# Token statistics of the first phase on ACT or DVE by the planner's queue ends, with a new pacing table

## The chip, the cores and the metric

The kernel runs on one core of one Trainium2 chip. The metric is the device time of one launch in microseconds; of a kernel, the median of its runs counts. Five engines work side by side, each through its own instructions in the order in which the program holds them: PE (TensorE, the matmuls, with its weight loads), DVE (VectorE), ACT (ScalarE), POOL (GpSimd), and SP, which here only issues DMAs. An instruction starts when those ahead of it on its engine are done and the semaphores that it waits for are there.

## What is computed

An input of 8192 tokens with 448 features is normalized over the features, and two branches start from the result: a spectral filter over the 8192 tokens (a real FFT, a small complex two-layer network on each frequency with a soft threshold behind it, the inverse FFT), and a GEGLU network of width 1792.

```
xn = (x - mean(x)) / sqrt(var(x) + 1e-5)          # per token, 448 features
s  = irfft2(soft(W2 . relu(W1 . rfft2(xn) + b1) + b2))   # 4 blocks of 112 features
g  = silu((gelu(xn @ w_gate) * (xn @ w_up)) @ w_down)
out = x + s * g
```

## The kernel before, in words

All of it is matmuls on 16-bit operands that are split in a high and a low part, so that three matmuls replace one of 32 bits. The FFT of 8192 is a product with 128x128 matrices, twiddles and a product over 64. The GEGLU products are done by a seven-product scheme (Strassen-Winograd) on halves of the operands.

**Stages.** The tokens go through the network in 16 chunks of 512, in two passes over the hidden width: pass 0 takes 8 of the 14 blocks of 128 hidden features, pass 1 takes 6. PE goes from one unit of the network to the next almost without a break from the start to the end. The work of the spectral branch is laid in between. Its first phase runs from about 84 to 640 us, one chunk of four token tiles (128 tokens each) every 34 us: `load_x` brings the tile `x4`, `stats` makes mean and variance per token in the tile `st`, `norm_act` normalizes on ACT, `factors` splits and adds up the operands of the seven products (scratch `sf` and `sx`, and `xs` for the plain halves) and stores them to `xts`, from which transposing DMAs bring them back as `xta` and `xtb` for the network, and `stage1` makes the first FFT product and stores it (`ysb` to `t1`). The second phase, to about 1450 us, is the middle of the spectral branch (tiles `va`, `vt`, `zs`, `t`), and the third, `load3` and `tiles3`, is the last inverse product: for each pair of token tiles it brings `u2`, `mt`, the input `x2` and the network's output `g2`, PE makes `bd <- u2,mt`, DVE multiplies the product into `g2`, DVE or POOL adds `x2`, and SP stores the result to `out`. The last chunk of the network takes the other way round: the inverse product waits in `s4`, and the network's own last step (`left`, then the silu on ACT into `th`, times `s4`, plus `x2`) ends with stores `out <- th`.

**Units.** A unit of the network handles two blocks of hidden features of a chunk. PE fills `bx` and `by` by products with `xta` (a1, a5, a6, a2 ...) and `xtb` (a3, a4); ACT copies (`by <- bx`, `u <- by`), DVE adds (`v <- bx,u`, `by <- bx,u`), ACT makes the gelu, and the results go as high and low 16-bit halves into `h`, on which the products with `dw` and `wt` (the down projection, into `bd`, `by` and `bx`) work. In pass 1 the weight tile `wt7` lends its space for the unit's 32-bit values, and `wt6` holds sums of halves of them: `wt <- wt` are the sums, `h <- wt,h` and `wt <- wt,wt` the low halves. 

**What sets the order.** Nothing in the program is ordered by hand. The order is written by a planner (`Pace`) while the program is built. It runs the parts above as coroutines against estimates: `cost` gives each operation a duration, `pace.free[e]` is the time at which the planner sees the queue of engine `e` end, and each instruction lands in its engine's queue at the moment when the planner reaches it. `calm(e)` holds a coroutine until the planner sees engine `e` free. `B` and `A` choose DVE or POOL, and ACT or POOL, by the earlier planned end. The table `STEPS` has a row for every stretch of planned time: its numbers are the allowance for a DMA's landing, how busy an engine may be for `calm` to pass, a factor on all costs of engines other than PE, a bias of the choices of `B` and `A`, and a factor on the distance at which groups of the second and tiles of the third phase are started. `SX`, the ring of `sx`, has two buffers, the ring of `g2` two, that of `th` three. SP's DMAs go over eight lanes, and each waits for the landing of the one eight before it.

`stats` is the function in which the code changes. Before, all four token tiles of a chunk go through `bn_stats` and `bn_aggr` on DVE; POOL makes the reciprocal root from the variances.

## Time and profile before

| | us |
|---|---|
| median of 3 runs | 1727.75 (1726.9 to 1728.06) |
| the profiled execution, its own time | 1729.31 |
| its span, first to last instruction | 1727.2 |
| PE busy | 1709.1 (99% of the span), 15654 matmuls |
| DVE busy | 1345.0 (78%), 2317 instructions |
| ACT busy | 1103.3 (64%), 2242 instructions |
| POOL busy | 1014.2 (59%), 1410 instructions |
| granted PE clock | 0.998 |

The profiled execution is 1.56 us above the median, and 2.1 us of its time lie outside its span. "Busy" is the time in which an engine executes instructions; the rest is waiting. In the chain of work that ended last PE has 87%, DVE 6%, and ACT, DMA and POOL 2% each.

### The profile page before, as it was taken

What the parts mean: (1) busy time and instruction counts of PE and PEld (TensorE: products, weight loads), DVE (VectorE), ACT (ScalarE), POOL (GpSimd) and SP (SyncE); (2) the same over time, 40 slices, a digit from 0 to 9 for tenths busy, and PEclk for the clock granted to TensorE, in tenths of its full rate; (3) what the DMA queues carried; (4) which work ended last, traced back from release to release, by engine and by line L of the source; (5) the groups of instructions that cost most, each with busy time, mean ns of one, the idle gap of its engine ahead of it and who ended that gap; (6) DMA issues with size and microseconds to landing.
All of it is one profiled execution on the core that took longest, in us unless ns stands there. A gap on an engine that the chain in (4) does not pass through costs nothing.

```text
span 1727.2 us, 41012 instructions
## 1 busy us (share of the span) xinstructions
PE 1709.1 (99%) x15654; PEld 1435.5 (83%) x15654; DVE 1345.0 (78%) x2317; ACT 1103.3 (64%) x2242; POOL 1014.2 (59%) x1410
## 2 busy tenths in 40 slices
PE   9999999999999999999999999999999999999998
PEld 4447677766777999998999999999999999889886
DVE  8998888778777878778786777787776786577776
ACT  6767766676756657678676667777676665333333
POOL 2487656677735785456374466654555654555556
PEclk9999999999999999999999999999999999999999
DMA  7348986997756753253535875454645544999996
GB/s 275 119 154 256 276 237 207 265 281 202 231 163 189 208 135 77 60 128 88 131 91 172 214 174 122 123 135 109 156 123 137 120 105 123 280 321 314 296 306 229
DMA packets 438308, 316.62 MB, mean 183 GB/s; under 512 B 305792, under 2 KB 409600, under 8 KB 436320
## 3 DMA queue, kind: packets, MB, share of 16 engines
q1 hardware_dynamic: 437824, 313.99, 64.4%
q8 instruction: 122, 2.00, 0.5%
q14 instruction: 74, 0.61, 0.1%
q10 hardware_dynamic: 288, 0.03, 0.0%
HBM read 137.93 MB, written 108.25 MB: 143 GB/s over the span
## 4 chain that ended last, share of the span: by engine, by line
PE 87%; DVE 6%; ACT 2%; DMA 2%; POOL 2%; issue 1%; SPq 0%; POOLq 0%; DVEq 0%; ACTq 0%
PE bd L290 35%; PE bx L290 30%; PE by L290 22%; DMA prt<-th 1%; DVE st L290 1%; ACT wt L290 1%; DVE raws L290 0%; POOL st L290 0%; DVE ysb L290 0%; DVE wt L290 0%; DVE dw L290 0%; DVE left L290 0%; DVE u L290 0%; DMA xta<-xts 0%; DVE h L290 0%
## 5 line engine op out<-in xcount | busy, mean ns | idle before, releaser
L290 PEld LDWEIGHTS <-wt 128*128 128x128 f16 x9142 | 885.4, 98 | 160.2 <-issue 8.2
L290 PE MATMUL bx<-xta,wt 128*128 128x256 f16 (+1 forms) x2819 | 354.0, 275 | 3.5 <-ACT by L290 2.6
L290 PEld LDWEIGHTS <-h 128*128 128x128 f16 x2711 | 259.8, 98 | 75.5 <-POOL h L290 1.6
L290 PE MATMUL by<-xtb,wt 128*128 128x256 f16 x2080 | 255.2, 273 | 0.4 <-DVE by L290 0.3
L290 PE MATMUL bd<-dw,h 128*128 128x448 f16 (+1 forms) x1536 | 243.1, 306 | 1.0 <-DVE ysb L290 0.7
L290 POOL TENSOR_TENSOR wt<-wt 128x256 f32<-128x256 f32 x181 | 140.2, 775 | 94.0 <-DVE wt L290 84.7
L290 PE MATMUL bx<-xtb,wt 128*128 128x256 f16 x1248 | 154.3, 274 | 2.2 <-DVE v L290 2.2
L290 PE MATMUL by<-xta,wt 128*128 128x256 f16 (+1 forms) x899 | 123.8, 282 | 0.1
L290 POOL TENSOR_TENSOR h<-wt,h 128x512 f16<-128x512 f32 (+1 forms) x92 | 96.1, 1058 | 35.9 <-ACT h L290 35.4
L290 DVE TENSOR_TENSOR by<-bx,u 128x512 f32<-128x512 f32 x104 | 72.4, 696 | 52.9 <-PE bx L290 44.9
L290 ACT ACTIVATE u<-by,fc 128x512 f32<-128x512 f32 (+1 forms) x118 | 73.6, 636 | 51.5 <-PE by L290 49.4
L290 PE MATMUL bx<-left,wt 128*128 128x256 f16 x816 | 99.9, 272 | 0.0
L290 DVE TENSOR_TENSOR v<-bx,u 128x512 f32<-128x512 f32 x104 | 71.4, 686 | 36.1 <-PE bx L290 35.5
L290 PE MATMUL bd<-dw,wt 128*128 128x224 f16 (+1 forms) x816 | 97.6, 264 | 0.5 <-DVE left L290 0.5
L290 POOL CAST zs<-t 112x256 f16<-112x256 f32 (+2 forms) x45 | 21.3, 474 | 123.1 <-DVE t L290 107.9
L290 ACT COPY u<-by 128x512 f32<-128x512 f32 x104 | 60.8, 585 | 50.2 <-PE by L290 49.4
L290 ACT CAST h<-wt 128x512 f16<-128x512 f32 (+1 forms) x128 | 68.5, 536 | 31.4 <-DVE wt L290 25.1
L290 PE MATMUL bd<-w2t,wn 113*128 113x112 f16 (+1 forms) x1152 | 77.6, 212 | 0.0
L290 ACT COPY by<-bx 128x512 f32<-128x512 f32 x104 | 59.8, 575 | 21.1 <-PE bx L290 20.8
L290 PE MATMUL bd<-wt,h 128*128 128x224 f16 x603 | 72.0, 259 | 0.8 <-POOL h L290 0.8
L290 PEld LDWEIGHTS <-wn 113*128 113x128 f16 (+1 forms) x1152 | 69.1, 97 | 2.1
L290 DVE SCALAR_TENSOR_TENSOR u<-by,fc,u 128x512 f32<-128x512 f32 (+1 forms) x86 | 55.2, 656 | 18.7 <-PE by L290 12.9
(283 smaller groups left out, 3764.8 us busy)
## 6 DMA issues: line engine op xcount, KB each, us to landing
xts<-sx SPq DMA_DIRECT2D x32, 480.0 KB, 3.6
x<-in_x SPq DMA_DIRECT2D x17, 896.0 KB, 6.2
t<-ysb SPq DMA_DIRECT2D x64, 224.0 KB, 3.8
prt<-th SPq DMA_DIRECT2D x64, 224.0 KB, 3.2
vt<-va SPq DMA_DIRECT2D x256, 56.0 KB, 2.1
left<-prt SPq DMA_DIRECT2D x64, 224.0 KB, 3.7
u<-t SPq DMA_DIRECT2D x32, 448.0 KB, 6.0
x<-in_x SPq DMA_DIRECT2D x32, 448.0 KB, 6.6
```

What stands on the lines that cost most here:

```text
L290: return self.pace.issue(self.name, kind, out, ins, lambda: fn(out, *args, **kw))
```

## The change

In `stats`, for each token tile, the planner compares the ends of two queues as it sees them. If ACT's end lies more than 0.6 us ahead of DVE's, the statistics of that tile are made on ACT: a Copy over the 448 features with a running sum (into `st`), a small Copy that scales it by -1/448, and a Square with that bias and a running sum, with a buffer of the ring `SX` as the place for the 448 results that nobody needs; two small operations on POOL scale the sums to mean and variance. Otherwise DVE does it as before.

```diff
@@ stats
         for a in range(CH):
+            if pace.free["ACT"] + 0.6 < pace.free["DVE"]:
+                sx = yield from SX.get()
+                yield from calm("ACT")
+                S.activation(sx[:, 0:D], x4[:, a, :], AF.Copy, accum_out=s6[:, a, 0:1])
+                S.activation(s6[:, a, 1:2], s6[:, a, 0:1], AF.Copy, scale=-1.0 / D)
+                yield
+                yield from calm("ACT")
+                S.activation(sx[:, 0:D], x4[:, a, :], AF.Square, bias=s6[:, a, 1:2], accum_out=s6[:, a, 2:3])
+                SX.put(sx)
+                G.tensor_scalar(mv[:, a, 0:1], s6[:, a, 0:1], 1.0 / D, None, op0=ALU.mult)
+                G.tensor_scalar(mv[:, a, 1:2], s6[:, a, 2:3], 1.0 / D, None, op0=ALU.mult)
+                yield
+                continue
             yield from (lull if c < PL else calm)("DVE")
             V.bn_stats(s6[:, a, :], x4[:, a, :])
             V.bn_aggr(mv[:, a, :], s6[:, a, :])
@@ STEPS, the rows up to 100 stay, of the others some two thirds differ
...
-(125, 2.5, 0.15, 1.04, 0.0, 1.0), (150, 2.5, 0.15, 1.04, 0.0, 1.0), (175, 2.5, 0.15, 1.04, 0.2, 1.0),
+(125, 2.5, 0.15, 1.07, 0.0, 0.9), (150, 2.5, 0.15, 1.07, 0.0, 0.9), (175, 2.25, 0.15, 1.04, 0.2, 1.0),
...
-(1725, 2.75, 0.05, 0.94, 0.4, 1.0)
+(1725, 1.25, 0.1, 1.045, -0.5, 1.06)
```

The program has the same 15654 matmuls and the same 886 DMAs. Of the 67 `bn_stats` and `bn_aggr` on DVE 44 each are left: 23 of the first phase's tiles go to ACT, which gains 23 of each of the three operations; POOL gains 46 small ones.

Because the planner now sees other times, the order changes on every engine. Three places show it. The first is ACT at the fifth `by <- bx` copy of the network, which before stands at 204.22 us. Before, in ACT's order, with the semaphores that each instruction waits for (`DMAHW` and a number is the landing on that lane; the number behind a name is that of the tile's copy):

```order
CAST wo<-wst 128x448 [waits DVE_49]
COPY by<-bx 128x512 [waits PE_49]
ACTIVATE ysb<-bd_69 128x2x224 [waits DMAHW5_49,DMAHW4_49,PE_49]
ACTIVATE x_1886,st<-x_1886,st 128x448
CAST wo<-wst 128x448 [waits DVE_49]
COPY u_2420<-by 128x512 [waits PE_49]
```

And now:

```order
ACTIVATE th<-bd_69,ms 128x448 [waits DMAHW4_49,PE_49]
ACTIVATE sx,st<-x_1916 128x448 [waits DMAHW7_49,DMAHW6_49,DMAHW3_49]
ACTIVATE st<-st 128x1 [waits Activation_49]
COPY by<-bx 128x512 [waits PE_49]
CAST wo<-wst 128x448 [waits DVE_49]
COPY u_2408<-by 128x512 [waits PE_49]
ACTIVATE sx,st<-x_1916,st 128x448 [waits Activation_49]
```

The first pass over the token tile now stands right ahead of the copy that PE needs, and it waits for three lanes: the load of `x4`, and the stores from the `sx` buffer that it takes over. Of the 23 first passes 13 wait for a DMA in this way.

The second place is POOL in the last unit of the network, from the last sums (`wt7 <- wt7`) to its end. Before:

```order
TENSOR_TENSOR wt7_83<-wt7_83 128x256 x4
TENSOR_TENSOR h_6804<-wt7_83,h_6804 128x512
TENSOR_TENSOR h_6804<-wt7_83,h_6804 128x256
TENSOR_TENSOR h_6804<-wt7_83,h_6804 128x512
TENSOR_TENSOR g2_24520<-g2_24520,x2_24486 128x448
TENSOR_TENSOR th_24607<-th_24607,x2_24210 128x448
```

And now:

```order
TENSOR_TENSOR wt6_82<-wt7_83,wt6_82 128x512
TENSOR_TENSOR h_6882<-wt7_83,h_6882 128x256
TENSOR_TENSOR th_24296<-th_24296,x2_24411 128x448
TENSOR_TENSOR wt6_82<-wt7_83,wt6_82 128x512
TENSOR_TENSOR g2_24426<-g2_24426,x2_24189 128x448
TENSOR_TENSOR wt7_83<-wt7_83 128x256 x3
TENSOR_TENSOR g2_24426<-g2_24426,x2_24189 128x448
TENSOR_TENSOR wt7_83<-wt7_83 128x256
TENSOR_TENSOR h_6882<-wt7_83,h_6882 128x256
TENSOR_TENSOR h_6882<-wt7_83,h_6882 128x512
```

POOL now also has both of the unit's `wt6` differences, which DVE had before, one addition into `th` and two into `g2` ahead of or among the last sums, and one of its last three `h` operations went to DVE. PE reads the last `h` in its products `bd <- wt,h`, 58 matmuls ahead of its end before, and a group of products earlier now.

The third place is DVE at its end, with SP's last stores. Before:

```order
SCALAR_TENSOR_TENSOR left_1744<-bd1_67,ms_86,left_1744 128x448
SCALAR_TENSOR_TENSOR left_1744<-bd0_66,ms_86,left_1744 128x448
TENSOR_TENSOR th_24719<-th_24719,s4_21439 128x448
SCALAR_TENSOR_TENSOR left_1744<-bx_24708,ms_86,left_1744 128x224
TENSOR_TENSOR th_24696<-th_24696,s4_21439 128x224 x2
```

And now:

```order
SCALAR_TENSOR_TENSOR left_1769<-bx_24787,ms_86,left_1769 128x224
SCALAR_TENSOR_TENSOR g2_24710<-bd0_66,ms_86,g2_24710 128x448
TENSOR_TENSOR th_24773<-th_24773,s4_21531 128x224
TENSOR_TENSOR th_24808<-th_24808,s4_21531 128x448
TENSOR_TENSOR th_24773<-th_24773,s4_21531 128x224
TENSOR_TENSOR th_24808<-th_24808,x2_24336 128x448
SCALAR_TENSOR_TENSOR g2_24710<-bd3_69,ms_86,g2_24710 128x448
TENSOR_TENSOR g2_24710<-g2_24710,x2_24629 128x448
```

Both `u2,mt` products of the last pair of tiles moved to PE's very end: one between the last nine products into `bx` (six of them ahead of it, three behind it), the other behind them as PE's last three matmuls, where before PE ended with `bx <- wt,h`. So DVE's last two operations now belong to `g2`, and SP's last DMA, which was a store `out <- th` of 128x224, is now the store `out <- g2` of 128x896.

## The prediction

> **What bounds the kernel now.** I read the busy times first, then PE's waits, then stretches of 100 us, and last the timeline around each place where PE stood still. The first lines of the page, and three rows of the windows (PE, PEld, DVE, ACT, POOL with the number of instructions, then granted clock, DMA share, GB/s):

> ```profile
> span 1727.2 us, 41012 instructions
> PE 1709.1 (99%) x15654; PEld 1435.5 (83%) x15654; DVE 1345.0 (78%) x2317; ACT 1103.3 (64%) x2242; POOL 1014.2 (59%) x1410
> ...
> 100.00:200.00 100.00, 97.14 (x629) 62.02 (x628) 88.16 (x168) 71.37 (x148) 75.12 (x133) 0.98 0.82 231
> 200.00:300.00 100.00, 98.56 (x779) 75.52 (x777) 85.66 (x153) 68.35 (x134) 62.96 (x108) 1.00 0.77 236
> 500.00:600.00 100.00, 100.00 (x851) 82.53 (x850) 80.55 (x168) 64.90 (x127) 56.16 (x98) 1.00 0.68 187
> ```

> PE is the bound: the change leaves its 15654 matmuls alone, so the time can only move in what PE waits and in what comes after its last matmul. The span has 18 us without PE (1727.2 - 1709.1). DVE is at 80 to 88% in the stretch of the statistics, ACT at 65 to 71%: both have room. PE's waits by cause:

> ```profile
> PE bx L290 <- ACT by L290: 2.6, 2, 1.9
> PE bx L290 <- DVE v L290: 2.2, 2, 1.4
> ...
> PE bd L290 <- POOL h L290: 1.1, 2, 0.8
> ...
> PE bd L290 <- DVE ysb L290: 0.7, 1, 0.7
> ```

> The rows left out, but for small ones, belong to the first 20 us, which the change leaves as they are. In the body stand `by` 2.6, `v` 2.2 and `ysb` 0.7: 5.5 us in five places, which is what there is to gain. `h` 1.1 is at the end.

> The sum is made against the profiled execution's own 1729.31 us (span 1727.2 and 2.1 outside); the median of the runs is 1727.75, so 1.56 is taken off again at the end. A change under 0.2%, 3.45 us, can hardly be told from none.

> **The statistics themselves.** What a token tile costs on each engine stands in rows of before; on ACT they are the same two passes that the kernel makes for another purpose at its start (the page of groups by form, window 23 to 100 us, and the answer on the tile `st`):

> ```profile
> L290 ACT ACTIVATE sx<-x,st 128x448 f16<-128x448 f32 x4 | 2.7, 668 | 0.1
> L290 ACT ACTIVATE sx<-x 128x448 f16<-128x448 f32 x4 | 2.3, 567 | 0.0
> ...
> L290 DVE BATCH_NORM_STATS2 st<-x x67: 593/615/628, 3.6 to 600.0; 128x6 f32<-128x448 f32 x67
> L290 DVE BATCH_NORM_AGGREGATE st<-st x67: 181/182/183, 4.3 to 600.7; 128x2 f32<-128x6 f32 x67
> L290 POOL TENSOR_SCALAR st<-st x44: 193/229/687, 4.6 to 603.8; 128x4 f32<-128x4 f32 x34, 128x1 f32<-128x1 f32 x8, 128x2 f32<-128x2 f32 x2
> L290 ACT ACTIVATE st<-st x9: 185/188/203, 9.7 to 37.6; 128x1 f32<-128x1 f32 x9
> L290 ACT ACTIVATION_READ_ACCUMULATOR sx<-x,st x4: 185/186/187, 25.6 to 38.4; 128x1 f32 x4
> ```

> DVE loses 0.615 + 0.182 = 0.797 us per tile. ACT gains 0.567 + 0.186 for the sum, 0.188 for the small Copy, 0.668 + 0.186 for the squares: 1.80 us. POOL gains 2 x 0.229 = 0.46. For 23 tiles that is DVE -18.3, ACT +41.3, POOL +10.5 us, spread over some 520 us. All of it lies beside PE. ACT rises from about 68% by 8 points (41.3 of 520 us), still under DVE, which falls by 3.5. As busy time I cost it at nothing; the cover is ACT's 30% of idle time.

> The price is in the waits. ACT works in order, and 13 of the 23 first passes wait for DMAs: for the load of `x4` and for the stores of the `sx` buffer that serves as scratch. Queued behind such a pass are the copies `by <- bx` and `u <- by` that PE waits for. Before has the like of it with another DMA, in ACT's and PE's timeline at 150 us, and among ACT's waits between 84 and 620 us:

> ```profile
> 150.24 0.63 ACT L290 ACTIVATE th<-bd,ms 128x448 f32<-128x448 f32 x1 [4.36 <-DMA prt<-th]
> 154.72 0.57 ACT L290 COPY by<-bx 128x512 f32<-128x512 f32 x1
> ...
> 155.35 0.92 PE L290 MATMUL bx<-xta,wt 128*128 128x256 f16 x7 [1.89 <-ACT by L290]
> ...
> ACT th L290 <- DMA prt<-th: 8.2, 3, 4.4
> ```

> ACT stood 4.36 us before a `th` whose buffer was still on its way out, the copy came late, and PE lost 1.89. Three `th` waited so, and one of the three cost PE. If about one or two of the 13 waits are late and one in three reaches PE, that is 0.6 us. The ends are 0 (the planner lets all of them come in time) and 3.8 (two such places). The old 1.89 itself stays: in the new order the same `th` waits for a store on a lane, ahead of the same copy.

> [...]

> **The order that moves with it, in the body.** Two of PE's places lose their cause. At 278 us and at 798 us:

> ```profile
> 273.96 3.42 DVE L290 SCALAR_TENSOR_TENSOR wst<-wst,rowc 128x128 f32<-128x128 f32 x1
> ...
> 278.72 0.68 DVE L290 TENSOR_TENSOR v<-bx,u 128x512 f32<-128x512 f32 x1
> 279.45 1.47 PE L290 MATMUL bx<-xtb,wt 128*128 128x256 f16 x12 [1.44 <-DVE v L290]
> ...
> 795.93 2.27 DVE L290 TENSOR_TENSOR wn<-h,wn 112x512 f16<-112x512 f32 x1
> 799.19 1.47 PE L290 MATMUL bx<-xtb,wt 128*128 128x256 f16 x12 [0.75 <-DVE v L290]
> ```

> In both a long DVE operation stood ahead of the `v` that PE waited for. In the new order the `wst` one stands behind that unit's `v`, and the `wn` one is not ahead of it: -1.44 and -0.75. What is late next there is nothing that I can see within half a microsecond. For `ysb` (0.7) I take half, since DVE has 18 us less to do and its order there is new: -0.35. The second `by` (2.6 - 1.9 = 0.7) and the 0.1 to 0.5 us places stay. Body: -1.44 - 0.75 - 0.35 + 0.6 = -1.9, with ends at -5.5 (all five places go) and +4 (two new ones, none goes). DMAs: the same 886 in another order on SP; their share in the first phase is 0.7 to 0.8, so I cost that at nothing, inside these ends.

> **The end of the program.** This term speaks against the change. The timeline of before, ACT, DVE and POOL from the last unit's `a4` on, PE's one wait, and its last matmuls:

> ```profile
> 1701.87 1.47 PE L290 MATMUL bx<-xtb,wt 128*128 128x256 f16 x12
> 1705.05 1.64 DVE L290 SCALAR_TENSOR_TENSOR wt<-v,fc,wt 128x512 f32<-128x512 f32 x1
> 1706.77 3.54 POOL L290 TENSOR_TENSOR wt<-wt 128x256 f32<-128x256 f32 x4 [0.63 <-DVE wt L290]
> 1710.39 3.33 POOL L290 TENSOR_TENSOR h<-wt,h 128x512 f16<-128x512 f32 x3
> 1713.69 1.51 POOL L290 TENSOR_TENSOR g<-g,x 128x448 f32<-128x448 f32 x1
> 1713.78 1.13 PE L290 MATMUL bd<-wt,h 128*128 128x224 f16 x10 [0.76 <-POOL h L290]
> 1720.20 0.45 PE L290 MATMUL bx<-wt,h 128*128 128x224 f16 x3
> 1721.39 1.48 DVE L290 TENSOR_TENSOR th<-th,s 128x224 f32<-128x224 f32 x2
> 1722.65 1.35 POOL L290 TENSOR_TENSOR th<-th,x 128x224 f32<-128x224 f32 x2 [0.33 <-DVE th L290]
> ```

> POOL's chain from the sums to the last `h` ends at 1713.72, 10.4 us behind `a4` (1703.34), and PE wanted it 0.76 earlier, at 9.6. In the new order POOL also has two additions into `g2`, one ahead of the sums and one among them (1.51 each, as in the row at 1713.69), and ahead of them a `th` and a `wt6`; one `h` of the three (3.33 / 3 = 1.1) is DVE's. I put one addition on the path, and 0.5 for what the others overrun POOL's idle 0.63: 1.51 + 0.5 - 1.1 = 0.9 later, 11.3 behind `a4`. PE has one group of products less in between (the 10 of 1713.78, 1.1) and wants it at 8.5. PE would stand 2.8 us where the two waits for `h` were 1.1 together: +1.7. Ends: +0.4 (the group alone, and the other of the two old waits and half of this one gone) and +2.3 (0.6 more, as when DVE is late with the product that the addition among the sums needs).

> Behind PE's last matmul (1720.65) before needed 6.55 us: `left`, `th`, POOL's addition, a store of 112 KB. In the new order DVE still has, after `left`, one `g2` multiply (0.68), three `th` (0.4, 0.63, 0.4), a `th` plus `x2` (0.63), then the last tile's `g2` multiply and addition (0.68 + 0.63). From 0.2 us ahead of PE's end that is 4.3 us behind it, where before the last store left 3.4 behind (1724.0, POOL's end). And the store is 448 KB, not 112:

> ```profile
> out<-g SPq DMA_DIRECT2D x2, 448.0 KB, 2.5
> out<-th SPq DMA_DIRECT2D x2, 112.0 KB, 1.7
> ```

> 0.9 and 0.8 make +1.7. The ends are +1.35 and +2.45; the upper one has the additions slow, as here, where the same 448 elements took 1.55 us beside POOL and 0.61 without it:

> ```profile
> 1703.07 1.58 POOL L290 TENSOR_TENSOR th<-th,x 128x448 f32<-128x448 f32 x1
> 1703.58 1.55 DVE L290 TENSOR_TENSOR g<-g,x 128x448 f32<-128x448 f32 x1
> ...
> 1709.11 0.61 DVE L290 TENSOR_TENSOR g<-g,x 128x448 f32<-128x448 f32 x1
> ```

> [...]

> **Sum.** -1.9 + 1.7 + 1.7 = +1.5. On the profiled execution's 1729.31 that is 1730.8; less the 1.56 by which it lies above the median, 1729.2: no change that can be told.

> **Rivals.** One, slower: the waits for the scratch buffer and `x4` decide. For it: 13 passes wait, each with PE's copies behind it, and the one such place shown cost 1.89. Against it: two of three late `th` cost PE nothing. It decides from two places on: 3.8 in place of the 0.6, the sum is +4.7 and the time 1732.4. The upper ends of the terms for the program's end (+4.75 in place of 3.4) bring the sum to +2.85 alone, and with one such place more (1.9) to +4.7 again.

> Two, faster: DVE's relief and the new order take away the five places of 5.5 us, nothing comes, and POOL's chain at the end costs only its lower end: -5.5 + 0.4 + 1.35 = -3.75, 1724.0. For it: 500 to 600 us ran with PE at 100.00 and DVE at 80.55, so a stretch of the statistics without a wait is possible. Against it: the 1.89 keeps its cause. If PE's end is met without POOL too, 1722.2.

> Three, nothing: the order is new and the waits are others of the same size, in the body and at the end; 1727.75. That the statistics don't move at all is excluded by the 23 tiles in the order.

> **How the numbers follow.** The forecast has 0.43 (its own range is 1726 to 1731), rival three 0.10, both inside 0.2%: same 0.53. Rival one and its kin 0.25, above 1731.2. Rival two 0.22, below 1724.3. The range leaves out a tenth on each side: below, half of rival two (1722.5), above, the body's two places with the upper ends at PE's end, less what is sure to go (1733.5).

> **What would show it.** ACT busy about 1145 us, DVE about 1327, POOL about 1025. PE's waits by `v` at 278 and 798 us gone, `by` at 153 us still there; a wait of PE for `h` of 2 to 3 us near its end; 8 to 8.5 us from PE's last matmul to the span's end, with a store of 448 KB as the last. Wrong is the forecast if ACT's `sx` rows show waits for DMAs of several microseconds with PE's `by` waits behind them, if PE's waits by `by`, `v` and `ysb` (5.5 us now) fall under 1 or rise over 8, or if PE meets `h` in time.

## The result, and the profile after

The changed kernel takes 1744.57 us (median of 4 runs, 1744.02 to 1745.72), before 1727.9 in the same comparison: a ratio of 1.0100, 95% interval 1.0085 to 1.0114. It is 16.7 us slower, where I had forecast no change with a range up to 1733.5. One execution of the last kernel below (2544.43 us at a granted clock of 0.65) is left out of that kernel's ratio. The head of its page:

```profile
span 1742.6 us, 41112 instructions
PE 1713.1 (98%) x15654; PEld 1435.8 (82%) x15654; DVE 1334.6 (77%) x2312; ACT 1129.2 (65%) x2353; POOL 1007.1 (58%) x1419
```

DVE lost 10.4 us of work, ACT gained 25.9, POOL lost 7.1, where the diff's own operations would make 18.3 less, 41.3 more and 10.5 more: the planner also moved other work between the engines. PE's matmuls are the same 15654. The 15.4 us between the two spans (1742.6 - 1727.2) are in PE's waits, in a lower clock behind some of them, and behind PE's last matmul. Between 84 and 1700 us PE stood still for 15.4 us, before for 6.7. The clock stood at half for 3.41 us twice, before once; each time takes 1.7 us of PE's work. The last unit has 1.5 us more of waiting, and 1.85 more lie behind the last matmul. Together that is 13.7; the remaining 1.7 us I can assign to no place. PE's waits by cause between 84 and 1700 us, the largest of after, then what before has below the rows of the prediction:

```profile
PE bd L290 <- DVE zs L290: 3.3, 2, 1.9
PE bd L290 <- ACT th L290: 2.9, 1, 2.9
PE bx L290 <- ACT by L290: 2.2, 3, 1.1
PE bx L290 <- DVE v L290: 2.1, 2, 1.5
PE bd L290 <- DVE xs L290: 1.1, 2, 0.7
PE bd L290 <- DVE h L290: 1.1, 2, 0.7
```

```profile
PE bd L290 <- DVE left L290: 0.5, 1, 0.5
PE bd L290 <- DVE zs L290: 0.3, 1, 0.3
PE by L290 <- DVE by L290: 0.3, 1, 0.3
```

After, the `th` row is new, and `zs` grew from 0.3 to 3.3. To see where the time goes I set the starts of PE's matmuls in the two traces against the same amount of PE work (columns streamed). After is ahead by 3.7 us when before stands at about 380 us: the waits at 153, 186 and 278 us became fewer, as hoped. It gives 3.2 of that back in small waits up to 550 us, loses 5.8 at one place (550 to 590 us) and 3.7 at another (around 881), about 3 in small pieces up to 1700, and 1.6 in the last unit: PE's last matmul is 13.5 us later.

The first place, ACT and PE in after's timeline, and the granted clock in the windows:

```profile
576.23 0.58 ACT L290 ACTIVATE sx<-x 128x448 f16<-128x448 f32 x1 [5.63 <-DMA xts<-sx]
578.58 0.67 ACT L290 ACTIVATE sx<-x,st 128x448 f16<-128x448 f32 x1
582.84 0.63 ACT L290 ACTIVATE th<-bd,ms 128x448 f32<-128x448 f32 x1
...
578.12 0.36 PE L290 MATMUL bd<-wt,h 128*128 128x224 f16 x2 [0.27 <-ACT h L290]
578.87 0.56 PE L290 MATMUL bd<-wt,h 128*128 128x224 f16 x4 [0.39 <-DVE h L290]
583.52 1.69 PE L290 MATMUL bd<-dw,left 128*128 128x224 f16 x12 [2.94 <-ACT th L290]
...
585.00:590.00 5.00, 5.00 (x37) 4.04 (x35) 3.04 (x7) 2.35 (x7) 3.46 (x9) 0.73 0.58 179
```

The first pass of the statistics on a token tile waited 5.63 us for the store from the scratch buffer that it takes over. Behind it on ACT stood the `h` casts, the `left` casts and the `th` copy that frees a bank for PE; PE stood 3.6 us in three waits, and behind them the clock fell. The 0.73 is a mean over the 5 us; cut where the clock changes, the windows show 0.50 for 3.41 us:

```profile
580.88:584.29 3.41, 0.77 (x9) 0.77 (x9) 3.02 (x7) 2.39 (x7) 3.26 (x10) 1.00 1.15 248
584.29:587.71 3.42, 3.42 (x20) 2.56 (x18) 2.75 (x6) 2.00 (x5) 3.17 (x6) 0.50 0.40 102
```

Two earlier first passes waited about a microsecond each for such a store, and PE waited behind both:

```profile
202.45 0.58 ACT L290 ACTIVATE sx<-x 128x448 f16<-128x448 f32 x1 [1.07 <-DMA xts<-sx]
203.89 1.25 PE L290 MATMUL bx<-xta,wt 128*128 128x256 f16 x10 [0.78 <-ACT by L290]
...
381.88 0.58 ACT L290 ACTIVATE sx<-x 128x448 f16<-128x448 f32 x1 [1.25 <-DMA xts<-sx]
386.07 1.25 PE L290 MATMUL bx<-xta,wt 128*128 128x256 f16 x10 [0.41 <-ACT by L290]
387.91 1.47 PE L290 MATMUL bx<-xtb,wt 128*128 128x256 f16 x12 [0.59 <-DVE v L290]
```

The program's end is near what the prediction's sum had: PE waits 1.17 for ACT's `h` and 1.17 for POOL's, and the last DMA is the `g2` store.

```profile
1723.72 0.36 PE L290 MATMUL bd<-wt,h 128*128 128x224 f16 x2 [1.17 <-ACT h L290]
1725.25 1.13 PE L290 MATMUL bd<-wt,h 128*128 128x224 f16 x10 [1.17 <-POOL h L290]
...
1739.06 0.34 SPq L290 DMA_DIRECT2D out<-g  x1
```

### The profile page after: what moved, and what is told of

Its sections match the earlier page's. It is cut to its first block, busy times and chain, and to the rows that moved or that the text cites. A ratio compares the mean times of both kernels' runs of the same rounds, so it can differ in the third digit from the quotient of the medians.

```text
span 1742.6 us, 41112 instructions
## 1 busy us (share of the span) xinstructions
PE 1713.1 (98%) x15654; PEld 1435.8 (82%) x15654; DVE 1334.6 (77%) x2312; ACT 1129.2 (65%) x2353; POOL 1007.1 (58%) x1419
## 4 chain that ended last, share of the span: by engine, by line
PE 77%; DVE 7%; POOL 3%; DMA 2%; ACT 2%; issue 2%; SPq 1%; ACTq 0%; DVEq 0%; POOLq 0%
PE bd L290 33%; PE bx L290 25%; PE by L290 18%; DMA xts<-sx 2%; DVE wt L290 1%; POOL wt L290 1%; SPq L290 1%; DVE h L290 1%; DVE left L290 1%; POOL h L290 1%; ACT sx L290 0%; DVE raws L290 0%; DVE sf L290 0%; DVE zs L290 0%; POOL sf L290 0%
## 5 line engine op out<-in xcount | busy, mean ns | idle before, releaser
L290 PEld LDWEIGHTS <-wt 128*128 128x128 f16 x9142 | 885.2, 98 | 158.6 <-issue 7.1
L290 PE MATMUL bx<-xta,wt 128*128 128x256 f16 (+1 forms) x2819 | 355.8, 276 | 3.0 <-ACT by L290 2.2
L290 PEld LDWEIGHTS <-h 128*128 128x128 f16 x2711 | 259.2, 98 | 81.4 <-POOL h L290 2.2
L290 PE MATMUL by<-xtb,wt 128*128 128x256 f16 x2080 | 254.3, 273 | 0.5 <-DVE by L290 0.5
L290 PE MATMUL bd<-dw,h 128*128 128x448 f16 (+1 forms) x1536 | 242.6, 306 | 0.8 <-DVE h L290 0.7
L290 POOL TENSOR_TENSOR wt<-wt 128x256 f32<-128x256 f32 x184 | 144.9, 788 | 106.9 <-DVE wt L290 96.3
L290 PE MATMUL bx<-xtb,wt 128*128 128x256 f16 x1248 | 153.4, 273 | 2.1 <-DVE v L290 2.1
L290 PE MATMUL by<-xta,wt 128*128 128x256 f16 (+1 forms) x899 | 123.8, 282 | 0.1
L290 POOL TENSOR_TENSOR h<-wt,h 128x256 f16<-128x256 f32 (+1 forms) x89 | 92.9, 1055 | 45.1 <-ACT h L290 42.0
L290 DVE TENSOR_TENSOR by<-bx,u 128x512 f32<-128x512 f32 x104 | 72.3, 695 | 54.3 <-PE bx L290 42.2
L290 ACT ACTIVATE u<-by,fc 128x512 f32<-128x512 f32 (+1 forms) x118 | 73.5, 635 | 41.7 <-PE by L290 40.7
L290 PE MATMUL bx<-left,wt 128*128 128x256 f16 x816 | 99.6, 273 | 0.0
L290 PE MATMUL bd<-dw,wt 128*128 128x224 f16 (+1 forms) x816 | 97.9, 264 | 0.2 <-DVE left L290 0.2
L290 DVE TENSOR_TENSOR v<-bx,u 128x512 f32<-128x512 f32 x104 | 71.3, 686 | 30.4 <-PE bx L290 29.4
L290 ACT COPY u<-by 128x512 f32<-128x512 f32 x104 | 60.7, 584 | 49.1 <-PE by L290 48.2
L290 ACT CAST h<-wt 128x512 f16<-128x512 f32 (+1 forms) x128 | 68.6, 536 | 30.9 <-DVE wt L290 25.1
L290 PE MATMUL bd<-w2t,wn 113*128 113x112 f16 (+1 forms) x1152 | 77.8, 212 | 0.8 <-DVE bd L290 0.8
L290 PE MATMUL bd<-wt,h 128*128 128x224 f16 x603 | 73.3, 259 | 3.2 <-ACT h L290 1.4
L290 ACT COPY by<-bx 128x512 f32<-128x512 f32 x104 | 60.0, 577 | 20.8 <-PE bx L290 20.6
L290 PEld LDWEIGHTS <-wn 113*128 113x128 f16 (+1 forms) x1152 | 69.2, 97 | 4.0 <-issue 1.1
L290 DVE SCALAR_TENSOR_TENSOR u<-by,fc,u 128x512 f32<-128x512 f32 (+1 forms) x86 | 55.3, 657 | 22.2 <-PE by L290 9.8
L290 PEld LDWEIGHTS <-w1t 112*112 112x112 f16 x612 | 66.5, 130 | 6.0 <-issue 3.9
## 6 DMA issues: line engine op xcount, KB each, us to landing
u<-t SPq DMA_DIRECT2D x32, 448.0 KB, 6.0
x<-in_x SPq DMA_DIRECT2D x32, 448.0 KB, 6.7
```

What stands on the lines that cost most here:

```text
L290: return self.pace.issue(self.name, kind, out, ins, lambda: fn(out, *args, **kw))
```

## The experiments

Two kinds of edit are used. Some change the planner's input, and with it the order of everything behind. Others hold the order: the planner is told the old operation, and only the instruction that is written differs, so that every other instruction stands where it stood. The code below is abridged; what stands behind `#` in it is a remark.

**The scratch buffer's stores.** Order held; the two passes write their unused results to a tile of 448 halves of their own.

```diff
+    junk = p1.tile([128, D], F16, name="junk")
-                S.activation(sx[:, 0:D], x4[:, a, :], AF.Copy, accum_out=s6[:, a, 0:1])
+                pace.issue("ACT", "activation", sx[:, 0:D], [x4[:, a, :], s6[:, a, 0:1]], lambda a=a: nc.scalar.activation(
+                    junk, x4[:, a, :], AF.Copy, accum_out=s6[:, a, 0:1]))
...
```

> The changed kernel with every instruction in the same place on every engine; only the two ACT passes of the statistics write their unused 448 results to a small tile of their own, so that they no longer wait for the stores from the sx buffer. The waits for x4's landing stay. Theory 1 (the wait of 5.63 us for a store at 570 us made ACT late and cost PE 2.94 + 0.39 + 0.27 us, and after it PE ran some microseconds at a granted clock of 0.73): these go, 5 to 7 us less, about 1738.5, and the clock from 585 to 590 us is 1.00. Rival (ACT was only the last of several that were late there; x4's landing or the network's transposed operand comes as late): under 1.5 us less, 1743 to 1745.

It took 1738.69 us (1.0055 of before, 1.0037 to 1.0072): 5.9 less than after. In its trace the same pass, and the windows of 5 us there:

```profile
572.33 0.58 ACT L723 ACTIVATE junk<-x 128x448 f16<-128x448 f32 x1 [2.97 <-DMA x<-in_x]
...
580.00:585.00 5.00, 5.00 (x50) 4.64 (x49) 3.00 (x7) 3.40 (x10) 4.34 (x11) 1.00 0.80 187
585.00:590.00 5.00, 5.00 (x54) 4.89 (x52) 2.69 (x6) 4.68 (x11) 1.41 (x3) 1.00 0.99 314
```

The wait for the store is gone, the one for the load of `x4` behind it remains (2.97), PE's wait at this place became 1.28, and the clock stays at 1.00. So the waits for the scratch buffer are shown to cost 5.9 us by the medians (6.8 if each kernel is set against before in its own comparison). The traces account for 5.8: 2.3 of PE's waits here (2.94 + 0.39 + 0.27 - 1.28), the 0.8 and the 1.0 at 204 and 387 us, which this kernel does not have, and 1.7 by the clock.

**And the slow subtraction on DVE.** The same kernel with one more instruction changed; order held.

```diff
+MOVE = {11082: 'POOL'}     # the subtraction into zs at 879 us
+            run = getattr(self.pace.real[to], op) if to else fn
```

> As the run before, and one instruction more changed: the subtraction into zs that took DVE 4.42 us at 879 us, beside five POOL operations in a row, is given to POOL, at the same place in the program. Theory 1 (DVE stood behind POOL's operations for a shared resource, and PE lost 1.92 us for it and then ran at a clock of 0.69): on POOL it takes about 0.7 us, PE's wait goes, 3 to 4.5 us less than the run before, about 1734.5. Rival (the operation is slow in itself, or POOL's own chain is what PE waits for next): within 1 us of the run before.

In after DVE took 4.42 us for what takes it about 0.42 at most other places, while POOL worked without a break:

```profile
879.07 4.42 DVE L290 TENSOR_TENSOR zs<-t,zs 112x256 f16<-112x256 f32 x1
...
879.00 0.72 POOL L290 TENSOR_TENSOR u<-u 128x256 f32<-128x256 f32 x1
879.68 1.16 POOL L290 TENSOR_TENSOR h<-u,h 128x512 f16<-128x512 f32 x1
880.79 1.30 POOL L290 TENSOR_TENSOR h<-gl,h 128x256 f16<-128x256 f32 x2
882.05 1.16 POOL L290 TENSOR_TENSOR left<-u,left 128x512 f16<-128x512 f32 x1
```

On POOL it took 0.67 us and PE's wait of 1.92 was gone, but two new ones stood behind it, and DVE's `left <- gl,left`, which took 0.41 us in after, now stood beside POOL's chain and took 3.17:

```profile
876.34 3.17 DVE L295 TENSOR_TENSOR left<-gl,left 128x256 f16<-128x256 f32 x1
...
888.98 0.67 PE L295 MATMUL bd<-w2t,wn 112*128 112x112 f16 x10 [0.64 <-POOL wn L295]
892.96 0.46 PE L295 MATMUL bd<-w2t,wn 113*128 113x112 f16 x6 [0.45 <-DVE bd L295]
```

By equal PE work the place is 2.3 us shorter. The time, 1738.18 us (1.0052, 1.0036 to 1.0068), is 0.5 less, which the noise hides and the rival's 1 us holds. The profiled execution was 1.2 us behind the other one before it came to the place, where the two kernels are alike, and it lost 1.6 more at the end, where the clock was 0.50 for 3.41 us behind the waits for `h`, which it had not been in the run before. The expectation of 3 to 4.5 us is a miss: PE's wait for `zs` went, most of the gain did not come.

**One part of the change alone.** First the table with the old `stats`, then the new `stats` with the old table.

```diff
# e_table: STEPS of after, stats of before
# e_branch: STEPS of before, stats of after
```

> The new pacing table with the statistics on DVE as before, a new order everywhere. Theory 1 (the loss comes from the statistics on ACT with their waits for the scratch buffer): no wait of PE over 2 us behind ACT in the first phase, at most half of the loss left, 1727 to 1736. Rival (the new table makes the loss, the statistics only happen to stand there): 1738 to 1746.

> The statistics by the planner's choice with the old pacing table; again 23 tiles go to ACT, 17 of the first passes wait for a DMA. Theory 1: ACT stands for microseconds before some of these passes, PE waits behind one or two of them, 1732 to 1742. Rival (the table makes the loss): within 0.2% of before, 1724.5 to 1731.5.

The table alone took 1750.96 us (1.0126, 1.0107 to 1.0145), the branch alone 1743.77 (1.0085, 1.0066 to 1.0104). The first is a miss for my first theory: with all statistics of the first phase on DVE as before, the loss is larger than in after. It lies above the rival's range too. The second lies above the range of the first theory and far above the rival's, which has no loss there. So each part alone loses about as much as the two together or more, and neither theory allows that. That made a second theory: it is not these edits that cost, but any new order.

**A neutral step.** Before, with one number of the table moved by a hundredth, so that nothing speaks for or against it; the order is the old one up to there and another behind.

```diff
-(125, 2.5, 0.15, 1.04, 0.0, 1.0), (150, 2.5, 0.15, 1.04, 0.0, 1.0)
+(125, 2.5, 0.15, 1.05, 0.0, 1.0), (150, 2.5, 0.15, 1.05, 0.0, 1.0)
# p_125b: 1.03;  p_675: rows 675 and 700, 1.03 -> 1.04;  p_1225: rows 1225 and 1250, 1.045 -> 1.055
```

> The kernel before with one number of the pacing table moved by a hundredth: the factor on the planner's costs in the rows 125 and 150 is 1.05 in place of 1.04. No statistics on ACT, no other change; the order is another from there on. Theory 2 (the order of before is one of many, kept because its stalls are few; any new order from 125 us on brings the usual number of stalls): 1734 to 1748. Rival (such a step means nothing by itself, and the losses of the runs so far come from the statistics on ACT or from the particular numbers of the new table): within 0.2% of before.

> The same with the rows 675 and 700, 1.04 in place of 1.03: the order is the same as before up to about 680 us and another behind it. Theory 2: about 60% of what a new order from 125 us on costs, 1731 to 1741, and no difference to before ahead of 670 us. Rival: within 0.2% of before.

> The same with the rows 1225 and 1250, 1.055 in place of 1.045: another order only in the last third. Theory 2: 1728 to 1736, the less the later the order parts. Rival: within 0.2% of before.

> The kernel before with the factor in the rows 125 and 150 of the table at 1.03, where before has 1.04 and an earlier run had 1.05: a second order from 125 us on that nothing speaks for or against. Theory 2 (before's order is the kept one of many): again 5 to 20 us more, 1733 to 1748. Rival (1.05 happened to be a bad number, 1.04 is no special one): 1724 to 1732.

| order new from | us | ratio to before, 95% interval |
|---|---|---|
| 125 us (1.05) | 1737.61 | 1.0060 (1.0043 to 1.0077) |
| 125 us (1.03) | 1740.88 | 1.0076 (1.0064 to 1.0089) |
| 675 us | 1734.43 | 1.0035 (1.0022 to 1.0048) |
| 1225 us | 1730.26 | 1.0011 (1.0002 to 1.0021) |

All four lie in the ranges of the second theory, the less the later the order parts. For 1225 us the rival's range, 0.2% around before, holds the result as well, so the first three decide. Where the time goes, in the windows: before, then the kernel that parts at 675 us.

```profile
100.00:640.00 540.00, 534.84 (x4134) 403.38 (x4133) 437.18 (x799) 365.15 (x722) 367.64 (x637) 1.00 0.76 219
1000.00:1400.00 400.00, 399.51 (x4199) 368.41 (x4197) 306.55 (x513) 280.38 (x575) 231.49 (x275) 1.00 0.52 129
```

```profile
100.00:640.00 540.00, 534.04 (x4139) 403.14 (x4138) 437.25 (x799) 365.44 (x723) 368.23 (x637) 1.00 0.77 219
1000.00:1400.00 400.00, 396.30 (x4165) 365.16 (x4163) 319.11 (x530) 280.21 (x571) 201.83 (x248) 1.00 0.54 130
```

Ahead of the parting the rows are alike, behind it PE waits 3.7 us in 400 where it waited 0.5. Between 84 and 1700 us PE waits 12.9 and 18.5 us in the two kernels that part at 125 us (1.05 and 1.03), 12.8 and 9.3 in the later ones, 6.7 in before and 15.4 in after. The waits are for the same kinds of results (`v`, `by`, `h`, `left`, `wn`), at other places; none of these four traces has a fall of the clock there.

**What a wait of PE costs.** Before, order held, with 4 to 20 useless ACT operations ahead of eight copies that PE waits for.

```diff
+PAD = {14308: 8, 14897: 16, 15626: 6, 16334: 12, 17042: 4, 17739: 20, 18395: 10, 19095: 14}
+            for _ in range(PAD.get(self.pace.calls, 0)):
+                self.pace.real["ACT"].activation(self.pace.junk, args[0][:, 0:64], AF.Copy)
```

> The kernel before, its order unchanged, with useless small operations on ACT ahead of eight copies by <- bx between 1096 and 1425 us (4 to 20 of them, each about 0.2 us), so that PE waits at eight places for about 0.8 to 4 us where it waits for nothing before. It tells what a wait of PE costs beside its own length. Theory (seen in the traces so far: after some waits of 1.9 us and more the granted clock is about 0.7 for 5 us): the waits up to 1.6 us cost their length, those from 2 us on cost 1 to 2 us more each by a lower clock; with some 18 us of waits the time is 18 + 5 = 23 us longer, about 1751. Rival (a wait costs its length, or less, since the planner's slack takes up some): 1740 to 1746, clock 1.00 throughout.

One run, 1737.31 us. Only three places gave long waits, since the copies had more room than I thought. Two of them are nearly alike (PE's waits, then windows of 5 us around each):

```profile
1138.84 0.49 PE L298 MATMUL bd<-z,w1t 112*112 112x256 f16 x3 [2.10 <-ACT h L298]
1338.60 1.51 PE L298 MATMUL bx<-left,wt 128*128 128x256 f16 x10 [2.04 <-ACT by L298]
...
1135.00:1140.00 5.00, 2.90 (x28) 2.31 (x27) 1.16 (x3) 4.65 (x17) 0.00 (x0) 1.00 0.49 140
1140.00:1145.00 5.00, 5.00 (x54) 4.64 (x53) 4.53 (x8) 4.58 (x10) 1.82 (x2) 1.00 0.03 6
1335.00:1340.00 5.00, 2.96 (x33) 2.55 (x31) 0.40 (x1) 4.63 (x17) 0.00 (x0) 0.95 0.64 178
1340.00:1345.00 5.00, 5.00 (x36) 3.89 (x35) 3.38 (x6) 3.24 (x7) 1.36 (x3) 0.71 0.00 0
```

Behind a wait of 2.10 us PE went on at full clock (54 matmuls in 5 us), behind one of 2.04 at a mean of 0.71 (36 matmuls). By equal PE work the first cost 2.3 us and the second 3.8. Neither side of the expectation is right: the length alone does not decide whether the clock falls. What goes with a fall shows when the windows are cut where the clock changes. In each of the twelve traces the clock's changes lie whole multiples of 3.413 us apart (in after they stand at 584.29, 587.71, 884.67 and 888.08 us), so the time can be divided into stretches of that length:

```profile
1134.66:1138.07 3.41, 2.08 (x21) 1.55 (x19) 1.07 (x2) 3.00 (x15) 0.00 (x0) 1.00 0.70 203
1138.07:1141.48 3.41, 2.64 (x25) 2.41 (x25) 1.58 (x3) 3.41 (x8) 0.00 (x0) 1.00 0.02 4
1336.05:1339.46 3.41, 1.36 (x18) 1.16 (x16) 0.40 (x1) 3.19 (x12) 0.00 (x0) 1.00 0.60 146
1339.46:1342.87 3.41, 3.41 (x22) 2.60 (x20) 2.25 (x4) 1.93 (x4) 0.93 (x2) 0.50 0.05 17
```

The wait of 2.10 us lies across two stretches, 1.33 us of it in one (3.41 - 2.08) and 0.77 in the next. The wait of 2.04 lies whole in one, and the next one runs at 0.50. From 84 us on all traces agree: the clock fell behind every stretch in which PE was idle, by the profile, for 1.89 us or more, and behind none with 1.64 or less; between the two lies no case.

**Single waits of before, taken away.** Order held but for four instructions in before.

```diff
+MOVE = {9888: 'POOL', 22623: 'DVE'}   # the wn subtraction at 796 us; one h of the last unit
+            if self.pace.calls == 1279:   # the th at 150 us, from ACT to DVE
+                ... tensor_scalar(out, args[0], kw["scale"], None, op0=ALU.mult)
+                if n == 2990:             # the h at 277 us, written behind the v at 278
+                    self.pace.held = lambda: run(out, *args, **kw)
```

> The kernel before with its order kept but for four instructions: the th at 150 us that waited for a store goes from ACT to DVE; at 278 us DVE makes v ahead of the h that stood ahead of it; at 796 us the subtraction into wn goes from DVE to POOL; in the last unit one of POOL's three h goes to DVE. Theory 2 (what is left to gain in this program is single waits of PE, and an edit that leaves the order alone gets them): PE's waits at 153 (1.89), 278 (half of 1.44), 798 (0.75) and 1713 us (0.76) go, and the low clock behind the first: 3 to 5.5 us less, about 1724. Rival (each such wait is followed by the next in line, as after the zs subtraction was moved): under 1.5 us less, 1726.5 to 1729.

1725.99 us, 0.9987 of before (0.9978 to 0.9997): 2.7 less by the medians, between the two expectations. Its largest waits of PE:

```profile
PE bx L302 <- ACT by L302: 1.6, 2, 0.9
PE bd L302 <- DVE ysb L302: 1.3, 1, 1.3
PE bd L302 <- POOL h L302: 0.5, 2, 0.3
```

`v` is gone, `by` fell from 2.6 to 1.6 and `h` from 1.1 to 0.5, while `ysb` rose from 0.7 to 1.3. Part of this is not the edit: in three other traces that still have before's order there (the padded kernel and the ones that part at 675 and 1225 us) the `by` at 155 us is 1.2 to 1.6 in place of 1.89, without a fall of the clock, and the `ysb` wait is 1.2. What the edit surely took away is the 2.2 of `v`. It is the only version here that is faster than before.

## Why the prediction was wrong

**The terms for the program's end came out, one of them in part by luck.** PE's waits there: 2.75 us in four pieces (0.21, 1.17, 1.17, 0.20), predicted 2.8. From PE's last matmul (1734.19) to the span's end 8.4 us, predicted 8.25, with the 448 KB store as the last DMA. Together 3.35 us more than before, against 3.4. POOL's last `h` ended 11.6 us behind `a4` where the sum had 11.3, so its mechanism holds, though half of PE's wait fell to ACT's `h`, which the sum does not name. Behind PE's last matmul two errors cancel: DVE ended 4.8 us behind it, not 4.3, as its three `th` took 2.6 us beside POOL where the sum has 1.43, and the store took 3.6, not 3.95.

```profile
1734.62 2.61 DVE L290 TENSOR_TENSOR th<-th,s 128x224 f32<-128x224 f32 x3
```

**The body failed**: -1.9 with ends at -5.5 and +4, measured about +12 (13.5 us by which PE's last matmul ends later, less 1.5 of more waiting in the last unit). Two steps of it are at fault.

The first is the price of the waits for the scratch buffer, rival one's mechanism: I put 0.6 us on it, with 3.8 as the end. It measured 5.9, most of it at one place of three. I had sized it by the one late `th` in before that cost PE 1.89, and 4.36 us of waiting on ACT reached PE as 1.89 with little queued behind. In after 5.63 us reached PE three times, since `h`, `left` and `th` stood behind the same pass. I also divided by three, because two of three late `th` had cost nothing; and one or two late places, of which one in three reaches PE, make 0.6 to 1.3 at 1.89 each, of which the sum took the lower end. Between 84 and 640 us ACT waited for stores from `sx` five times, 8.4 us in all, and the three waits over 1 us all reached PE. The clock had no term at all, though the prediction's own row of 100 to 200 us has 0.98: at the place at 580 us it cost 1.7.

```profile
ACT sx L290 <- DMA xts<-sx: 8.4, 5, 5.6
```

The second, and the larger, is the step "Two of PE's places lose their cause", with the other small places put as staying. I compared the new order with the waits that the old one had, took off those whose cause was gone, and let the rest of the program be as it was. They did go: PE waits for no `v` at 278 or 798 us, and after leads by 3.7 us at 380. But the body of before is one order of many, with 6.7 us of PE waiting in 1600; after has 15.4. The neutral steps show what another order has: 9.3 and 12.2 us more when it is new from 125 us on. Without the scratch buffer's stores after is 10 us over before, which lies among those. That the rest of after's loss is nothing but this is argued from the sizes, not shown place by place, and that before's order was once kept because its stalls are few is an inference; no run shows how it was found. Rival three, "the waits are others of the same size", had the right mechanism and the wrong size; its side should have been the slow one.

**Smaller points.** I said that the 1.89 at 153 us stays; it went, while other waits for `by` of up to 1.1 came. As a number it was high: with the order unchanged other executions have 1.2 to 1.6 there. Rival two's 1722.2 is nearer 1722.5 by its own terms (-5.5 - 1.1 + 1.35). ACT rose to 1129.2 us, not 1145, DVE fell to 1334.6, not 1327, and POOL fell to 1007.1 where I had 1025: the planner sent other work elsewhere. ACT's longer time per tile (1.80 us against 0.80) was hidden; it was ACT's place in front of PE's copies that cost. That a DVE operation can take long beside POOL's work deserved more weight: the subtraction took 4.42 us beside POOL's chain in after, and 0.67 on POOL. In the body I had no term for it, though the prediction's own rows have 3.42 us at 274 us, and POOL worked without a break there too, from 270.04 to 278.25. At the program's end I had slow additions in the upper end only (1.55 us against 0.61), and the three `th` took 2.6 us for the sum's 1.43.

## What to carry to other kernels

When a kernel's order was picked for few stalls, cost an edit that reorders it by what another, neutral order costs, not by the old order's waits: runs with a meaningless step of a tuning number measure that. In an in-order queue that serves the bound engine, count what stands behind an instruction that waits for a DMA, and give scratch results a buffer that no transfer reads. Edits that hold the order and change single instructions are small, but two of the three here gained (5.9 and 2.7 us); the gain of the third was lost in the noise and in the waits next in line.
